# Plain chunks 9 to 7, pairs 19 to 20, weight sums from the second chunk on, and some early transfers moved

## The chip, the cores and the metric

The kernel runs on one core of one Trainium2 chip. Its time is the device time in microseconds (us) of one execution. Before the change it is 2727.89 us, the median of three runs (2726.22 to 2728.48). The core has five engines that run at the same time, each with its own queue of instructions in a fixed order: TensorE (PE, matmuls), VectorE (DVE), ScalarE (ACT), GpSimd (POOL) and SyncE (SP, which here only issues DMAs). POOL issues DMAs as well, from its own queue.

## What is computed

Eight sequences of 3008 tokens with 256 channels go through a Fourier transform along the sequence, a complex 256x256 mix with soft thresholding of the spectrum, the inverse transform, and a gated feed-forward network (256 to 1536 to 256) on all 24064 tokens.

```python
X = np.fft.rfft(x, axis=1)
Yr = Xr @ w_r - Xi @ w_i + b_r
Yi = Xr @ w_i + Xi @ w_r + b_i
Y = sign(Y) * maximum(abs(Y) - 0.01, 0)        # real and imaginary part apart
y = np.fft.irfft(Y, n=3008, axis=1).reshape(24064, 256)
gate = 1 / (1 + np.exp(-(y @ w_gate)))
out = (gate * (y @ w_val)) @ w_out
```

## The kernel before, in words

**FFT.** 3008 is 47 x 64, so the transform is two stages with a store to DRAM and a load between them. Stage one is `fwd_a` for one of eight row groups of a batch (a *first-stage unit*: load `xf`, matmuls, copy, store to `zd`; `store_a` issues the store as two DMAs of 192 KB). Stage two, mix and inverse stage one run in *steps* `(q, b)`: `fwd_b(q)`, `mix(q - 1)`, `inv_b(q - 2)`. A step loads `zf` and a table `mf_sb`, and an inverse table `mi_sb` (two buffers, `NME`). Inverse stage two is `inv_a(u)`, an *inverse unit*: it loads `vf` and gives 376 tokens. The batches go in groups of 1, 1, 2, 2, 2 (`GROUPS`).

**Feed-forward network, plain.** The first T0 = `NPL` x 512 tokens go in chunks of 512 (`CW`). A chunk has 12 *units* (`ffn1`, `ffn2`; f is a block of 128 of the 1536 hidden features). A unit is 12 matmuls of 512 columns for gate and value (each a three-term product of high and low halves) and 6 for the output of an earlier unit: 18. On VectorE it has two operations (L465, L474), on ScalarE two (L463, L473).

**Feed-forward network, in pairs.** The other tokens go two chunks at a time (`half`, `second`): the gate and value products are made as 2x2 block products with 7 in place of 8 multiplications. A pair has 12 halves of 7 x 3 matmuls and 12 x 12 for the output. This needs sums of weight blocks, which `make_t` makes on POOL: 12 passes, each with two buffers of the ring `big` (five buffers, shared with `xf` of the first stage) and a store to `td`.

**Order.** The first block (manual order) transforms batch 0, converts weights and starts batch 1. Chunk 0 runs in manual order beside the first stage of batches 2 and 3 (`halves`) and the rest of the weight conversion. From chunk 1 on, a list `side` holds the remaining FFT work (steps, first-stage and inverse units, with weights such as 3.6 for a full step and 1.0 for a first-stage or inverse unit). After every unit the pace `rates` is added to `acc`, and side work is taken from the list as long as `acc` covers its weight. All of `side` but the last sixteen inverse units is spread over the units from 12 up to `len(ffn) - LAST_GAP` (20). Outside the manual blocks a scheduler orders each engine's instructions. Matmul results go to a ring of six PSUM banks (`RING`). At the end of the last chunk the FFT's buffers are given up, and the pairs start.

A VectorE step is, by line: L287 and L290 (operand of the mix), L308, L312, L313 (sum after the mix), L296 (threshold, after ScalarE's L295) and L319 (low half, after ScalarE's L318).

Of the kernel before, what the change touches and what calls it, by code (L numbers as in the profile page):

```python
# [22 lines left out]
LAM = float(np.float32(0.01))  # L23
GROUPS = (1, 1, 2, 2, 2)
CW = 512
NPL = 9
HW = 512
RING, L2_BANKS = 6, 2

# [8 lines left out]
EARLY = 4  # L38
# [71 lines left out]
def tile_fft_mix_ffn(ctx: ExitStack, tc, x, w_r, w_i, b_r, b_i, w_one, w_out, mf, mi, mis, fa, fb, mf0, fa0, out):  # L110
    nc = tc.nc
# [819 lines left out]
    def load_halves(b, u):  # L931
        for c in range(2):
            load_half(b, 2 * u + c)
# [11 lines left out]
    with tc.manual_schedule():  # L945
        for h in range(na):
            load_a(0, h)
        load_a(1, 0)
        for h in range(na):
            fwd_a(0, h)  # L950
            store_a(0, h)
            if h in (1, 3, 4):
                load_a(1, {1: 1, 3: 2, 4: 3}[h])
            if h == 2:
                load_mix()
        mfs[0] = load_mf(0, mf0)
        for q in range(2):
            load_b(0, q)
        mfs[1] = load_mf(1, mf0)
        load_bias4()  # L960
        load_part()
        mfs[2] = load_mf(2, mf0)
        for h in range(EARLY):
            fwd_a(1, h)
            if h == 1:
                wi_sb = mix_weights()
        keep_warm(bank("warm"), zero[:, :P], zero, WARM_Z)
        for q in range(NP + 2):
            if q + 2 < NP:
                load_b(0, q + 2)  # L970
            if 0 <= q - 1 < NP:
                mis_[q - 1] = load_mi(q - 1, True)
            if q < 2:
                for h in range(q * EARLY // 2, (q + 1) * EARLY // 2):
                    store_a(1, h)
            if q == 3:
                nc.sync.dma_start(fb_sb, fb)
                load_bias()
            if q % 2 and q <= NP:
                load_part()  # L980
            if q % 2 == 0 and 4 <= q < 4 + 2 * (na - EARLY):
                load_a(1, EARLY + q // 2 - 2)
            if q < NP:
                fwd_b(0, q, mfs[q], True)
            if q + 3 < NP:
                mfs[q + 3] = load_mf(q + 3, mf0)

            if q < NP:
                convert(q)
            if q == 4:  # L990
                sub(bias_sb[:, 1], bias_sb[:, 1], bias_sb[:, 0])
            if 0 <= q - 1 < NP:
                mix4(0, q - 1)
            if q == NP + 1:
                for bu in beside[:NR2K // 2]:
                    load_halves(*bu)
            if 0 <= q - 2 < NP:
                inv_b(0, q - 2, mis_[q - 2], True)
        steps = [convert_a, convert_b, convert_c]
        for h in range(EARLY, na):  # L1000
            fwd_a(1, h)
            store_a(1, h, nc.gpsimd)
            if steps:
                steps.pop(0)()
        for bu in beside[:AT_FIRST]:
            halves_a(*waiting.pop(0))
        for t in ("hi lo", "power mant one", "sum word", "hi lo"):
            ops(t, 0)
    p0s.close()
    p3 = p3s.enter_context(tc.tile_pool(name="p3", bufs=2, side="right", reuse_waits="tile"))  # L1010
    with tc.manual_schedule():
        for u in own0:
            load_v(u)
        load_part()
        for bu in beside[NR2K // 2:NR2K // 2 + AT_FIRST]:
            load_halves(*bu)
        for f in range(NF):
            ffn[f]()
            if parts:
                load_part()  # L1020
            if f in (2, 3):
                tables[f - 2, 1] = load_mi(f - 2, False, later=True)
            if f in (5, 6):
                keep_mi(f - 5, tables[f - 5, 1])
            halves(AT_FIRST + (f + 1) * (len(beside) - AT_FIRST) // NF)
# [49 lines left out]
    for j in range(NF, len(ffn)):  # L1075
        c, f = divmod(j, NF)
        ffn[j]()
        acc += rates[j >= part]
        if ts and c >= 3 and f % 4 == 1:
            make_t(*ts.pop(0))  # L1080
        while side and (acc >= side[0][0] or j >= (part if len(side) > n_last else end) - 1):
            if len(side) == n_last and j < part:
                break
            acc -= side[0][0]
            side.pop(0)[1]()
            if len(side) == n_last:
                fft.close()
                p4 = ctx.enter_context(tc.tile_pool(name="p4", bufs=1, reuse_waits="tile"))
                th, tl = (p4.tile([P, NH, 2, 3, P], F32R, name=t) for t in ("th", "tl"))
                spare += [p4.tile([P, 2, HW], F32R, tag="xop", bufs=NCB, name="spare") for _ in range(BEHIND)]  # L1090
                prep = list(PREP)
                to_load = list(range(NH))
                acc = 0.0
        if p4 and to_load and j % 2:
            load_t(to_load.pop(0))
        if c == NPL - 1:
            if f == 0:
                load_y(0)
            if f % 2:
                load_t1(f // 2)  # L1100
            if prep and f > 2:
                operand(0, prep[0])
                split(0, prep.pop(0), sub)
# [74 lines left out]
```

## Time and profile before

| | before |
|---|---|
| median of 3 runs | 2727.89 us |
| profiled execution, its own time | 2728.32 us |
| its span, first to last instruction | 2726.2 us |
| mean granted clock of TensorE | 0.997 |
| DMA packets, data | 170552, 241.48 MB |
| HBM read, written | 134.19 MB, 104.33 MB |

The busy time of each engine in 40 slices of the span, in tenths (9 is 90% or more), shows the stages: up to slice 2 the start, up to slice 15 the plain chunks with the FFT beside them, then the pairs.

```profile
PE   8899999999999999999999999999999999999999
DVE  5777778677777448777777777777777877777776
ACT  4666565555555444444444444444444444444443
POOL 0231001216000003333333324333333333333321
DMA  9887645777555660000000000000000000000000
```

The 1.0 for a full TensorE clock and the DMA share are means over a window; a wait is the idle time of an engine just before an instruction, put down to what released it last.

### The profile page before, as it was taken

How to read it: one execution, taken by the hardware profiler on the slowest of the kernel's cores; microseconds unless marked ns; L12 is line 12 of the kernel's file. 1: busy time of each engine (PE TensorE's matmuls, PEld its weight loads, DVE VectorE, ACT ScalarE, POOL GpSimd, SP SyncE). 2: the span in 40 equal slices, each digit the busy share in tenths (PEclk: the TensorE clock that was granted, in tenths of full speed). 3: DMA queues.
4: the chain of work that ended last, by engine and by line, in shares of the span. 5: the costliest groups of instructions: out<-in, count | busy, mean ns of one | idle time of the engine just before them, and what ended most of it. 6: DMA issues, size and time to landing. Idle time of an engine off the chain costs nothing.

```text
span 2726.2 us, 45298 instructions
## 1 busy us (share of the span) xinstructions
PE 2702.6 (99%) x17371; PEld 2240.3 (82%) x17371; DVE 2041.4 (75%) x3013; ACT 1353.3 (50%) x2373; POOL 727.8 (27%) x673
## 2 busy tenths in 40 slices
PE   8899999999999999999999999999999999999999
PEld 6668888888899888888888888888888888888887
DVE  5777778677777448777777777777777877777776
ACT  4666565555555444444444444444444444444443
POOL 0231001216000003333333324333333333333321
PEclk9999999999999999999999999999999999999999
DMA  9887645777555660000000000000000000000000
GB/s 279 256 247 200 185 136 173 205 211 213 167 161 155 191 182 9 31 31 16 16 31 32 16 16 31 31 26 7 31 32 31 2 31 31 31 16 16 32 16 16
DMA packets 170552, 241.48 MB, mean 89 GB/s; under 512 B 17184, under 2 KB 127648, under 8 KB 170336
## 3 DMA queue, kind: packets, MB, share of 16 engines
q1 hardware_dynamic: 159664, 215.18, 26.3%
q0 software_dynamic: 10416, 23.34, 2.7%
q8 instruction: 137, 2.24, 0.4%
q14 instruction: 79, 0.65, 0.1%
q10 hardware_dynamic: 256, 0.07, 0.0%
HBM read 134.19 MB, written 104.33 MB: 87 GB/s over the span
## 4 chain that ended last, share of the span: by engine, by line
PE 95%; DMA 2%; DVE 2%; ACT 1%; issue 0%; SPq 0%; POOL 0%; ACTq 0%; DVEq 0%
PE pc L717 11%; PE pd L717 11%; PE pa L717 11%; PE po L693 8%; PE po L692 8%; PE po L694 8%; PE pm L306 6%; PE pb L717 6%; PE pb L272 3%; PE pia L393 2%; PE pg L457 2%; PE pg L458 2%; PE pg L459 2%; PE pv L457 2%; PE po L485 2%; PE pv L458 2%
## 5 line engine op out<-in xcount | busy, mean ns | idle before, releaser
L775 POOL TENSOR_TENSOR c<-c,c 128x512 f32<-128x512 f32 x114 | 147.3, 1292 | 779.2 <-DVE c L771 588.4
L692 PE MATMUL po<-hh,w 128*128 128x512 f32 x912 | 354.8, 389 | 0.0
L693 PE MATMUL po<-hh,w 128*128 128x512 f32 x912 | 354.8, 389 | 0.0
L694 PE MATMUL po<-hl,w 128*128 128x512 f32 x912 | 354.8, 389 | 0.0
L717 PE MATMUL pc<-s,w1h 128*128 128x512 f32 x912 | 280.9, 389 | 0.0
L717 PE MATMUL pa<-a,w1h 128*128 128x512 f32 x912 | 280.8, 389 | 0.0
L771 DVE TENSOR_TENSOR c<-u,pc 128x512 f32<-128x512 f32 x228 | 156.7, 687 | 91.1 <-PE pc L717 85.3
L746 DVE TENSOR_TENSOR u<-u,pb 128x512 f32<-128x512 f32 x228 | 155.4, 681 | 91.2 <-PE pb L717 61.2
L664 ACT CAST hh<-v 128x512 fp32r<-128x512 f32 x114 | 70.7, 620 | 305.7 <-DVE v L756 305.7
L668 POOL TENSOR_TENSOR hl<-c,hh 128x512 fp32r<-128x512 f32 x114 | 152.4, 1337 | 186.1 <-ACT hh L664 186.1
L717 PEld LDWEIGHTS pc<-s,w1h 128*128 128x128 f32 x912 | 171.1, 188 | 35.7 <-DVE v L748 0.2
L692 PEld LDWEIGHTS po<-hh,w 128*128 128x128 f32 x912 | 171.2, 188 | 35.6
L694 PEld LDWEIGHTS po<-hl,w 128*128 128x128 f32 x912 | 171.2, 188 | 35.6
L717 PEld LDWEIGHTS pa<-a,w1h 128*128 128x128 f32 x912 | 171.2, 188 | 35.6
L693 PEld LDWEIGHTS po<-hh,w 128*128 128x128 f32 x912 | 171.2, 188 | 35.4
L306 PE MATMUL pm<-w_sb,xsh 128*128 128x256 f32 x1008 | 187.2, 287 | 1.2 <-ACT xsh L289 0.8
L717 PE MATMUL pc<-s,w1l 128*128 128x512 f32 x456 | 177.4, 389 | 0.0
L717 PE MATMUL pa<-a,w1l 128*128 128x512 f32 x456 | 177.4, 389 | 0.0
L750 DVE TENSOR_TENSOR v<-v,pd 128x512 f32<-128x512 f32 x228 | 156.8, 688 | 24.4 <-DVE v L748 0.9
L777 DVE TENSOR_TENSOR u<-u,pd 128x512 f32<-128x512 f32 x228 | 156.8, 688 | 24.5 <-DVE c L771 0.9
L748 DVE TENSOR_TENSOR v<-u,pc 128x512 f32<-128x512 f32 x228 | 156.8, 688 | 24.1 <-PE pd L717 0.5
L742 ACT COPY u<-pa 128x512 f32<-128x512 f32 x228 | 133.9, 587 | 70.2 <-PE pa L717 70.0
(185 smaller groups left out, 6620.7 us busy)
## 6 DMA issues: line engine op xcount, KB each, us to landing
zf<-zd SPq DMA_DIRECT2D x96, 256.0 KB, 3.4
vf<-vd SPq DMA_DIRECT2D x128, 192.0 KB, 3.9
out_dram<-ot SPq DMA_DIRECT2D x93, 256.0 KB, 2.2
vd<-vz SPq DMA_DIRECT2D x85, 256.0 KB, 2.9
ypair<-yd SPq DMA_DIRECT2D x19, 1024.0 KB, 4.9
yd<-yf SPq DMA_DIRECT2D x103, 188.0 KB, 3.4
xf<-in_x_dram SPq DMA_DIRECT2D x80, 192.0 KB, 4.4
zd<-xf SPq DMA_DIRECT2D x72, 192.0 KB, 2.9
```

The lines of the kernel that those rows point to most:

```text
L306: nc.tensor.matmul(o, l, r, start=(i == 0), stop=(i == len(mms) - 1))
L668: sub_(hl, h, hh)
L692: nc.tensor.matmul(o, wh, hh, start=(f == 0), stop=False)
L693: nc.tensor.matmul(o, wl, hh, start=False, stop=False)
L694: nc.tensor.matmul(o, wh, hl, start=False, stop=(f == NF - 1))
L717: nc.tensor.matmul(o, l, r, start=not more and l is wh and r is xh, stop=l is wl, skip_group_check=more)
L746: add(u, u, b)
L748: add(v, u, c)
L750: add(v, v, d)
L771: add(c12, u, c)
L775: nc.gpsimd.tensor_mul(c12, g12, c12)
L777: add(u, u, d)
```

## The change

```diff
-NPL = 9
+NPL = 7
...
-            if 0 <= q - 1 < NP:
-                mis_[q - 1] = load_mi(q - 1, True)
+            for i in (0, 1) if q == 1 else (q - 1,) if 2 < q <= NP else ():
+                mis_[i] = load_mi(i, True)
...
         for h in range(EARLY, na):
             fwd_a(1, h)
-            store_a(1, h, nc.gpsimd)
+            if h == EARLY:
+                store_a(1, h, nc.gpsimd)
             if steps:
                 steps.pop(0)()
...
         for bu in beside[NR2K // 2:NR2K // 2 + AT_FIRST]:
             load_halves(*bu)
+        for h in range(EARLY + 1, na):
+            store_a(1, h)
         for f in range(NF):
             ffn[f]()
...
-        if ts and c >= 3 and f % 4 == 1:
+        if ts and c >= 1 and f % 4 == 1:
             make_t(*ts.pop(0))
```

There are 7 plain chunks (84 units) and 20 pairs, where there were 9 (108 units) and 19. The side work up to the last sixteen inverse units, with weights of 369.4 in sum (372.4 after: three inverse units move from the chunks' own list to it), is spread over 52 units, where it was 76: `rates` is 372.4 / 52 = 7.16 a unit, where it was 369.4 / 76 = 4.86. Passes of `make_t` follow units 13, 17, 21 and so on to 57, where they followed 37, 41 and so on to 81. In the first block the tables `mi_sb` of q = 0 and 1 are loaded together. The stores of three first-stage units of batch 1 (h = 5, 6, 7) move from POOL to SP, behind the first loads of chunk 0.

SyncE, at the start of chunk 0, in the change against before (`xfh` is the input of `halves`, `vf` that of an inverse unit, `raw` a piece of the weights to be converted, `zd_84` the first-stage result of batch 1):

```order
 L865 DMA raw<-in_w_out_dram 128x1024
 L168 DMA xfh<-in_x_dram 48x512 x4
+L168 DMA zd_84<-xf 48x1024 x6
 L168 DMA vf<-vd_91 48x1024 x2
 L865 DMA raw<-in_w_one_dram 128x1024
```

The six stores are new on SP here; on POOL, `zd_84<-xf` falls from eight to two.

VectorE in the FFT of batch 1, before: from one unit of the network (L465) to the next.

```order
L465 TENSOR_TENSOR sg<-sg,pv 128x512
L296 SCALAR_TENSOR_TENSOR yc<-ys,yc 128x512
L474 TENSOR_TENSOR hl<-sg,hh 128x512
L319 TENSOR_TENSOR yl<-yc,yh 128x512
L287 TENSOR_TENSOR xsf<-xsf 128x2x128
L308 TENSOR_TENSOR yt<-pm,bias_sb 128x512
L290 TENSOR_TENSOR xsl<-xsf,xsh 128x768
L312 TENSOR_TENSOR ys<-pm_2289,yt 64x256
```

The same place in the change; the rows begin inside the first of two steps.

```order
L287 TENSOR_TENSOR xsf<-xsf 128x2x128
L308 TENSOR_TENSOR yt<-pm,bias_sb 128x512
L296 SCALAR_TENSOR_TENSOR yc<-ys,yc 128x512
L290 TENSOR_TENSOR xsl<-xsf,xsh 128x768
L319 TENSOR_TENSOR yl<-yc,yh 128x512
L312 TENSOR_TENSOR ys<-pm_2448,yt 64x256
L313 TENSOR_TENSOR ys<-yt 64x256
L312 TENSOR_TENSOR ys<-pm_2448,yt 64x256
L313 TENSOR_TENSOR ys<-yt 64x256
L296 SCALAR_TENSOR_TENSOR yc<-ys,yc 128x512
L319 TENSOR_TENSOR yl<-yc,yh 128x512
L465 TENSOR_TENSOR sg<-sg,pv 128x512
```

Two steps now stand between two units, where one stood, and L313, L296 and L319 of the second step follow each other directly, with a ScalarE operation between each two of them.

GpSimd in the change, among the inverse tables of the second FFT (`mi_sb` loaded, then kept in `md`; `tb` and `tr` are the buffers of `make_t`):

```order
L253 DMA mi_sb<-in_mis_dram 128x2x256
L588 TENSOR_TENSOR tb<-w1h,w1l 128x256 x2
L590 TENSOR_TENSOR tb<-tb 128x128
L591 TENSOR_TENSOR tb<-tb 128x128
L592 TENSOR_TENSOR tb<-tb 128x128
L593 TENSOR_TENSOR tb<-tb 128x128
L259 DMA md<-mi_sb 128x2x256
L253 DMA mi_sb<-in_mis_dram 128x2x256
```

Before, all tables stand ahead of the first `tb`; now one pass lies between two of them, and the one of unit 13 lies among the stores of chunk 0.

## The prediction

> **What bounds the kernel now.** I read the page first (engine shares, chain), then TensorE's (PE's) own waits, then two windows: the stage in which FFT steps run between the plain units, and the stage of the pairs.
>
> ```profile
> span 2726.2 us, 45298 instructions
> PE 2702.6 (99%) x17371; PEld 2240.3 (82%) x17371; DVE 2041.4 (75%) x3013; ACT 1353.3 (50%) x2373; POOL 727.8 (27%) x673
> PE 95%; DMA 2%; DVE 2%; ACT 1%; issue 0%; SPq 0%; POOL 0%; ACTq 0%; DVEq 0%
> ...
> PE pia L393 <- issue: 3.2, 1, 3.2
> PE pia L393 <- DMA vf<-vd: 2.4, 3, 1.4
> PE pi L348 <- DMA mi_sb<-in_mi_dram: 1.8, 2, 1.6
> ...
> 640.00:670.00 30.00, 30.00 (x306) 25.15 (x299) 24.34 (x33) 16.19 (x30) 23.38 (x36) 1.00 0.68 209
> 670.00:700.00 30.00, 29.56 (x359) 24.61 (x358) 23.64 (x39) 17.74 (x34) 11.89 (x19) 1.00 0.80 227
> 700.00:730.00 30.00, 29.37 (x355) 25.86 (x354) 20.11 (x36) 17.11 (x30) 0.00 (x0) 1.00 0.59 165
> 190.00:905.00 715.00, 713.73 (x7083) 614.62 (x7083) 547.18 (x930) 422.57 (x734) 101.34 (x152) 1.00 0.62 178
> 1400.00:2000.00 600.00, 600.00 (x2649) 496.82 (x2648) 471.56 (x643) 271.43 (x473) 206.85 (x155) 1.00 0.06 22
> ```
>
> The window columns are PE, weight loads, VectorE (DVE), ScalarE (ACT), GpSimd (POOL), clock, DMA share, GB/s. PE is busy all the way and makes 95% of the chain, so a matmul less is time less, as long as nothing else becomes late. In the pairs 2649 matmuls take 600 us: **0.2265 us each**. The rows of waits (total, times, longest) are small, and those shown lie in the first 110 us: a table, an input of the first inverse units, and an unexplained `issue`. In the plain stage (190 to 905 us) PE is busy 713.73 of 715. VectorE comes second there, 547 us; it is the engine to watch when that stage is squeezed.
>
> **Two plain chunks become a pair.** A plain chunk issues 12 x 18 = 216 matmuls of 512 columns, two of them 432. A pair issues 12 halves x 7 products x 3 = 252 and 12 x 12 = 144 for the output, 396. So 36 fall away: 36 x 0.2265 = **-8.15 us**. The FFT, its inverse and the weight sums keep their number of instructions.
>
> **The two inverse tables.** PE waits for the second table after its operand is long ready:
>
> ```profile
> 49.73 0.45 PE L348 MATMUL pi<-yc,mi_sb 128*128 128x256 f32 x1 [1.58 <-DMA mi_sb<-in_mi_dram]
> ```
>
> It is issued behind four stores; moved ahead of them, some 5 us earlier, it lands before PE asks for it. These stores, one raw load and a table behind them go out later by one issue, some 0.5 us, and nobody waits for them there. Bounds 0 and -1.8 (both waits of that row's kind); I take **-1.6**.
>
> **The six stores (three units).** They leave POOL at 98 to 102 us, while the first inverse units wait for their input:
>
> ```profile
> 98.15 2.07 POOL L168 DMA_DIRECT2D zd<-xf  x4 [1.09 <-ACT xf L203]
> 101.45 1.02 POOL L168 DMA_DIRECT2D zd<-xf  x2 [1.24 <-ACT xf L203]
> ...
> zd<-xf SPq DMA_DIRECT2D x72, 192.0 KB, 2.9
> ...
> 100.00:110.00 10.00, 4.56 (x133) 3.61 (x132) 5.34 (x10) 5.14 (x10) 3.25 (x7) 0.70 0.98 325
> 110.00:120.00 10.00, 10.00 (x52) 6.32 (x52) 5.68 (x11) 6.79 (x12) 2.21 (x4) 0.79 0.43 123
> ...
> 102.60 1.15 PE L393 MATMUL pia<-fb_sb,vf 48*64 48x47 f32 x64 [1.44 <-DMA vf<-vd]
> 104.08 1.74 PE L393 MATMUL pia<-fb_sb,vf 48*64 48x47 f32 x54 [0.33 <-DMA vf<-vd]
> 109.03 0.46 PE L393 MATMUL pia<-fb_sb,vf 48*64 48x47 f32 x6 [3.22 <-issue]
> 109.96 0.80 PE L457 MATMUL pg<-yth,w1h 128*128 128x512 f32 x1 [0.46 <-ACT yth L381]
> 116.00 0.50 PE L457 MATMUL pg<-yth,w1h 128*128 128x512 f32 x1
> 120.09 0.50 PE L457 MATMUL pg<-yth,w1h 128*128 128x512 f32 x1
> ```
>
> Six transfers of 192 KB are 1.2 MB, 3.6 us at the 325 GB/s of that window. DMA is full (0.98) until 110 us and half empty (0.43) behind it; the stores now go out on SP at about 104 to 108 us, into that gap. Of the three PE waits here, 1.44 and 0.33 are for that input and 3.22 for nothing the profile shows (my reading: the next instructions, fetched through the same DMA). The first unit then takes 6.04 us (109.96 to 116.00), the second 4.09, at a clock of 0.79. Bounds: +3.7 if SP's next loads slip by as much as the stores take and PE waits for it, and -7 for all waits and the slow clock gone. I take the two input waits and a third of the 3.22: **-3.0**.
>
> The Trainium skill (TensorE: Matmul & The Clock Gate, "What's actually happening") says that the clock halves after one idle window of about 3.4 us; the 0.70 and 0.79 agree. By it the slow first unit, 2 us, would go too once the waits are short, and the sum would be 2 us lower; by the rows alone I leave it in.
>
> **The plain stage gets denser.** The 84 full FFT steps that lay between 76 units now lie between 52: the pace at which the kernel hands out side work rises from 4.86 to 7.16 of its weights a unit, so that a unit is followed by two steps where it was one. The stage loses 24 units, 24 x 4.08 = 98 us, of PE cover, and the side work keeps its size. PE's costs come from the starts of three units in a row: between the first two lie a unit, a step and a first-stage unit, between the last two a unit and a step. DVE's come from its groups in the window (busy and mean, then the idle time ahead and who ended it):
>
> ```profile
> 411.40 0.39 PE L457 MATMUL pg<-yth,w1h 128*128 128x512 f32 x1
> 420.45 0.40 PE L457 MATMUL pg<-yth,w1h 128*128 128x512 f32 x1
> 428.27 0.40 PE L457 MATMUL pg<-yth,w1h 128*128 128x512 f32 x1
> ...
> L290 DVE TENSOR_TENSOR xsl<-xsf,xsh 128x768 fp32r<-128x768 f32 x84 | 83.1, 989 | 8.7 <-ACT xsh L289 7.9
> L313 DVE TENSOR_TENSOR ys<-yt 64x256 f32<-64x256 f32 x168 | 77.1, 459 | 3.7
> L312 DVE TENSOR_TENSOR ys<-pm,yt 64x256 f32<-64x256 f32 x168 | 70.6, 420 | 7.8
> L296 DVE SCALAR_TENSOR_TENSOR yc<-ys,yc 128x512 f32<-128x512 f32 x84 | 59.7, 711 | 54.2 <-ACT yc L295 53.5
> L319 DVE TENSOR_TENSOR yl<-yc,yh 128x512 fp32r<-128x512 f32 x83 | 58.8, 708 | 26.9 <-ACT yh L318 26.4
> L308 DVE TENSOR_TENSOR yt<-pm,bias_sb 128x512 f32<-128x512 f32 x84 | 57.8, 688 | 10.1 <-PE pm L306 9.1
> L474 DVE TENSOR_TENSOR hl<-sg,hh 128x512 fp32r<-128x512 f32 x75 | 52.3, 698 | 20.9 <-ACT hh L473 20.1
> L465 DVE TENSOR_TENSOR sg<-sg,pv 128x512 f32<-128x512 f32 x75 | 51.6, 688 | 10.3 <-PE pv L459 4.3 <-ACT sg L463 3.8
> L287 DVE TENSOR_TENSOR xsf<-xsf 128x256 f32<-128x256 f32 x83 | 38.0, 457 | 24.0 <-ACT xsf L285 23.3
> ```
>
> On PE a unit is 18 x 0.2265 = 4.08 us, a step 7.82 - 4.08 = 3.74, a first-stage unit 9.05 - 7.82 = 1.23; an inverse unit I take as 1.1, from the row of 64 small matmuls at 102.60 (1.15). On DVE a step is the seven FFT groups, 445.1 / 84 = 5.30, a unit (L474, L465) 1.39; the groups add up to 563 with the small ones, the window has 547, so neighbours overlap by 3%: 5.15 and 1.35. Besides, DVE stands idle where it hands a tile to ACT and takes it straight back (L296, L319, L474): 102 us on the 133 places where the order leaves nothing between, 0.77 each. Before: 547 + 102 = 649 of 715, 91%. After, units 13 to 33 hold 36 steps, 18 first-stage and 9 inverse units and 44 such places: PE 85.7 + 134.6 + 22.1 + 9.9 = 252; DVE 185 + 28 + 4 + 34 = 251. Units 34 to 64 (48 steps, 14, 37, 67 places): PE 364, DVE 347. So for 250 us DVE has nothing to spare, and what hid it, PE's longer row of matmuls, is gone. PE is not stopped at once: its results lie in six PSUM banks, and an order with some slack in it takes up a short lead of one engine. But a lead that grows ends in PE waiting for a bank or for a split operand. The nearest place in the trace is 640 to 700 us, where GpSimd's sums slow DVE (24 of 30 busy): PE lost 0.44 and 0.63 us in 60 to 90. Over 252 us that is 3 to 4.5. Bounds 0 and +13 (rival 3); I take **+4.5**.
>
> **The weight sums** run from the second chunk on, five of twelve passes in units 13 to 33. What they cost DVE is in the means above. POOL also loads the second FFT's tables:
>
> ```profile
> 651.22 1.86 POOL L588 TENSOR_TENSOR tb<-w1h,w1l 128x256 f32<-128x256 f32 x2
> 659.51 1.44 POOL L588 TENSOR_TENSOR tb<-w1h,w1l 128x256 f32<-128x256 f32 x2
> ...
> 659.16 2.09 DVE L313 TENSOR_TENSOR ys<-yt 64x256 f32<-64x256 f32 x1
> ...
> POOL mi_sb L253 <- PE pi L353: 39.5, 10, 12.7
> ```
>
> One pass takes 8.3 us there (from one start to the next). In the order one lies between the tables of the second FFT, and one among the first chunk's stores. Behind it on POOL wait a table and its copy, and for the table PE's inverse product. POOL has 4 us in hand per table (39.5 over 10, waiting for a free buffer), and a table is asked for two steps, 7.5 us, after it could be issued; two passes could cost PE at most 2 x (8.3 - 4.0) = 8.6. DMA, busy 0.62 of 715 us, comes to 0.72 of 617 (715 - 98); at 0.80, in the row 670 to 700, PE lost 0.44. I take **+1.5** for both, near the lower end of 0 to +8.6, since the step ahead covers most of a pass.
>
> The Trainium skill (GPSIMD Engine Reference, "8. Key points") says that POOL shares its SBUF interfaces with DVE instructions of two SBUF inputs. The 2.09 us against a mean of 459 ns agrees that there is contention. What it would cost at its worst is rival 4; by the means of the groups it is inside the 5.15 and 1.35, and the sum stays as it is.
>
> **Sum.** -8.15 - 1.6 - 3.0 + 4.5 + 1.5 = -6.75. The profiled execution took 2728.32 us (2.1 around its span); 2728.32 - 6.75 = 2721.6. The median, 2727.89, lies 0.4 lower: **2721 us**.
>
> **Rivals.**
> 1. DVE keeps up and the start clears: -8.15 - 1.6 - 7 + 0 = 2711. For it: before, PE waited only some 3 us in 715. Against: no spare time in units 13 to 33.
> 2. The stores' move gains nothing (SP's loads slip, or the 3.22 stays): -8.15 - 1.6 + 0 + 6 = about 2724, no change to be told. That is the change not doing what it says. For it: the 3.22 has no named cause, and SP is a queue in order, whose next loads feed the first chunk.
> 3. Slower: DVE becomes the bound in units 13 to 33. If each place of direct return grows by 0.3 us, since ACT, at most 422.57 / 617 = 68% busy, is more often in the middle of another tile, 44 x 0.3 = 13 come on top: 2734. It decides (slower by more than 0.2%) from 12.2 / 44 = 0.28 us on. Against: the mean, 54.2 us over 67 places, is 0.81 with ACT at 59%.
> 4. Slower by more: GpSimd's sums stop DVE for as long as they run. Five passes of 8.3 us in the full units are 41 us: about 2762. Against: from 640 to 670 us POOL was busy 23.38 and DVE still 24.34 of 30.
>
> **How the numbers follow.** Forecast 0.40, of which 0.30 lies below 2722.4, the bound of 0.2% (5.5 us, about what a measurement of this kernel can tell from no change); rival 1 0.22; rival 2 0.23; rival 3 0.13, of which 0.02 within 0.2%; rival 4 0.02. Faster 0.30 + 0.22 = 0.52, same 0.10 + 0.23 + 0.02 = 0.35, slower 0.11 + 0.02 = 0.13. The range, 2711 to 2733, runs from rival 1 to just short of rival 3, and leaves out half of either end.
>
> **What would show it.** Right: no wait for the second table; less than 4 us of PE waits at 100 to 110 us; PE waits of 3 to 8 us in units 13 to 33, ended by DVE; 20 pairs at 89.7 us each. Wrong: PE waits there above 15 us or none; loads of tables waited for behind POOL's sums; new waits for loads in the first chunk.

## The result and the profile after

The changed kernel is slower: 2745.18 us, median of six runs (2743.36 to 2751.2), beside 2729.28 us for the kernel before on the same chip (six runs as well, the three shown ahead among them); ratio 1.0065, 95% interval 1.0054 to 1.0076. The profiled execution has a span of 2743.9 us, 17.7 us more than before.

The page of the changed kernel: span, busy time, two rows of the 40 slices, and the chain.

```profile
span 2743.9 us, 45406 instructions
PE 2708.0 (99%) x17335; PEld 2241.8 (82%) x17335; DVE 2072.8 (76%) x3052; ACT 1358.9 (50%) x2390; POOL 753.5 (27%) x690
...
DVE  5777777777883577778777777777777777787776
...
POOL 0242120221000133333333333333433333333321
...
PE 87%; DVE 7%; ACT 3%; DMA 2%; issue 1%; SPq 0%; POOL 0%; DVEq 0%; ACTq 0%
```

PE still looks 99% busy, but its share of the chain fell from 95% to 87%, and VectorE's (DVE's) rose from 2% to 7%: for some 5% more of the time than before, the end is set by DVE's work. GpSimd's (POOL's) peak of 6 tenths in slice 9 before (counted from 0) is now spread over slices 3 to 9.

PE's own waits in the same profile (total, times, longest):

```profile
PE pi L351 <- ACT yh L318: 6.6, 6, 2.8
...
PE pia L393 <- issue: 2.8, 2, 2.0
PE pb L272 <- DMA zf<-zd: 2.4, 2, 1.3
PE pm L306 <- DVE yt L308: 2.3, 1, 2.3
```

The same row in the plain stage of the kernel before (190 to 905 us):

```profile
PE pi L351 <- ACT yh L318: 0.3, 1, 0.3
```

The largest wait is new, 6.6 us in the whole run, 5.9 of them from 188 us on: the inverse product (L351) waits for the high half of the thresholded spectrum (L318), a link near the end of the chain of a step through DVE and ScalarE (ACT). These rows explain only part of the loss. The ends of matmuls are modelled, so a short gap between two of them is partly painted over, and after a longer one the clock is lower. I therefore measured each unit by its start: **time over the matmuls** is the time from a unit's first gate matmul to the next unit's, less the matmuls that the program puts between at their own durations (us each, fitted to units 14 to 85 before: network 0.2305, mix 0.1146, inverse product 0.1234, first FFT product 0.2396, first stage 0.288, an inverse unit 1.2).

| us over the matmuls | start of unit 13 | units 13 to 20 | 21 to 33 | 34 to 44 | 45 to 64 | later units | sum |
|---|---|---|---|---|---|---|---|
| before | 190.68 | 0.0 | 2.1 | 0.0 | 0.9 | 3.7 | 6.5 |
| changed | 188.35 | 16.5 | 8.8 | 1.0 | 8.9 | 0.8 | 35.9 |

From the last plain unit's start to the end of the span it is 1716.8 us before and 1806.9 after, so the pair that was added takes 90.2; the 24 plain units that went took 24 x 18 x 0.2305 = 99.6. Together: 90.2 - 99.6 = -9.4, the start -2.3, the FFT stage 35.9 - 6.5 = +29.4, in sum +17.7, which is the difference of the spans. The loss is all in units 13 to 64.

How such a loss arises, in the timeline of the changed kernel (start, duration, engine, operation, then the idle time before it and who ended it):

```profile
214.17 1.94 DVE L313 TENSOR_TENSOR ys<-yt 64x256 f32<-64x256 f32 x1
...
214.38 1.44 POOL L588 TENSOR_TENSOR tb<-w1h,w1l 128x256 f32<-128x256 f32 x2
...
216.12 0.43 DVE L312 TENSOR_TENSOR ys<-pm,yt 64x256 f32<-64x256 f32 x1
...
217.17 0.73 ACT L295 ACTIVATE yc<-ys,ebias 128x512 f32<-128x512 f32 x1 [2.29 <-DVE ys L313]
...
218.38 0.68 DVE L296 SCALAR_TENSOR_TENSOR yc<-ys,yc 128x512 f32<-128x512 f32 x1
...
219.09 0.62 ACT L318 CAST yh<-yc 128x512 fp32r<-128x512 f32 x1 [0.47 <-DVE yc L296]
...
219.76 0.39 PE L351 MATMUL pi<-yh,mi_sb 128*128 128x256 f32 x1 [1.77 <-ACT yh L318]
```

L313, 0.42 us elsewhere, takes 1.94 while POOL makes two of its sums. L312, which reads PSUM, keeps its 0.43. ACT then waits 2.29 us for L313, and PE 1.77 us for ACT. The windows of such places (PE, weight loads, DVE, ACT, POOL, clock, DMA share, GB/s):

```profile
206.60:225.30 18.70, 16.93 (x97) 12.19 (x94) 13.44 (x21) 8.69 (x15) 6.38 (x11) 0.86 0.66 195
...
611.40:627.30 15.90, 13.42 (x148) 12.06 (x148) 12.95 (x16) 6.57 (x13) 14.18 (x24) 1.00 0.77 238
```

DVE is not full in the first (13.44 of 18.70), and the clock falls to 0.86; in the second POOL works for 14.18 of 15.90 us, and 16 DVE operations take 12.95.

### The profile page after: what moved, and what is told of

It is laid out like the page before. It is cut to its first block, busy times and chain, and to the rows that moved or that the text cites. A ratio compares the mean times of both kernels' runs of the same rounds, so it can differ in the third digit from the quotient of the medians.

```text
span 2743.9 us, 45406 instructions
## 1 busy us (share of the span) xinstructions
PE 2708.0 (99%) x17335; PEld 2241.8 (82%) x17335; DVE 2072.8 (76%) x3052; ACT 1358.9 (50%) x2390; POOL 753.5 (27%) x690
## 3 DMA queue, kind: packets, MB, share of 16 engines
q1 hardware_dynamic: 161680, 218.46, 26.4%
q0 software_dynamic: 10032, 22.16, 2.5%
## 4 chain that ended last, share of the span: by engine, by line
PE 87%; DVE 7%; ACT 3%; DMA 2%; issue 1%; SPq 0%; POOL 0%; DVEq 0%; ACTq 0%
PE pa L717 12%; PE pc L717 12%; PE pd L717 12%; PE po L694 8%; PE po L693 8%; PE po L692 8%; PE pb L717 6%; PE pm L306 4%; PE pb L272 2%; PE pia L393 2%; PE pg L457 1%; PE pa L201 1%; PE pg L458 1%; PE pv L457 1%; PE pg L459 1%
## 5 line engine op out<-in xcount | busy, mean ns | idle before, releaser
L692 PE MATMUL po<-hh,w 128*128 128x512 f32 x960 | 373.5, 389 | 0.0
L693 PE MATMUL po<-hh,w 128*128 128x512 f32 x960 | 373.5, 389 | 0.0
L694 PE MATMUL po<-hl,w 128*128 128x512 f32 x960 | 373.4, 389 | 0.0
L717 PE MATMUL pa<-a,w1h 128*128 128x512 f32 x960 | 295.7, 389 | 0.0
L717 PE MATMUL pc<-s,w1h 128*128 128x512 f32 x960 | 295.6, 389 | 0.0
L717 PEld LDWEIGHTS pa<-a,w1h 128*128 128x128 f32 x960 | 180.1, 188 | 37.7 <-DVE sg L465 0.4
L717 PEld LDWEIGHTS pc<-s,w1h 128*128 128x128 f32 x960 | 180.1, 188 | 37.6 <-DVE v L748 0.2
L692 PEld LDWEIGHTS po<-hh,w 128*128 128x128 f32 x960 | 180.2, 188 | 37.4
L693 PEld LDWEIGHTS po<-hh,w 128*128 128x128 f32 x960 | 180.2, 188 | 37.4
L694 PEld LDWEIGHTS po<-hl,w 128*128 128x128 f32 x960 | 180.2, 188 | 37.4
L306 PE MATMUL pm<-w_sb,xsh 128*128 128x256 f32 x1008 | 187.3, 287 | 3.3 <-DVE yt L308 2.3
L717 PE MATMUL pa<-a,w1l 128*128 128x512 f32 x480 | 186.8, 389 | 0.0
L717 PE MATMUL pc<-s,w1l 128*128 128x512 f32 x480 | 186.8, 389 | 0.0
```

The costliest lines, as they stand in the source:

```text
L306: nc.tensor.matmul(o, l, r, start=(i == 0), stop=(i == len(mms) - 1))
L692: nc.tensor.matmul(o, wh, hh, start=(f == 0), stop=False)
L693: nc.tensor.matmul(o, wl, hh, start=False, stop=False)
L694: nc.tensor.matmul(o, wh, hl, start=False, stop=(f == NF - 1))
L717: nc.tensor.matmul(o, l, r, start=not more and l is wh and r is xh, stop=l is wl, skip_group_check=more)
```

## The experiments

Three theories stood against each other. A: the results of a step pass DVE and ACT for longer than a step takes on PE, and where two steps of one and the same batch stand between two units, PE comes too early. B: DVE is full. C: the arithmetic of the weight sums stops DVE. Line numbers of the later kernels are a few higher than those of the change (L307 for L306, L353 for L351). The table gives each run's time and its time over the matmuls, as above; the ratios with their intervals stand with the runs. Each row is one profile. The run with the start as before, whose plain stage is that of the change, has a sum of 32.0 us in place of 35.9, so some 4 us between two rows can be scatter.

| kernel | us, median | start of unit 13 | units 13 to 20 | 21 to 33 | 34 to 44 | 45 to 64 | later | sum |
|---|---|---|---|---|---|---|---|---|
| sums' arithmetic out (e2) | 2735.86 | 197.94 | 8.3 | 2.6 | -0.9 | 4.9 | 0.7 | 15.5 |
| the same, buffers kept (f2) | 2729.83 | 192.79 | 8.3 | 3.7 | -0.9 | 3.7 | 0.9 | 15.8 |
| slower pace for batch 1 (e3) | 2745.70 | 190.75 | 2.6 | 5.7 | 5.1 | 19.5 | 0.4 | 33.3 |
| both (g1) | 2733.28 | 187.15 | 0.0 | 2.8 | 1.0 | 17.8 | 0.3 | 22.0 |
| both, loads earlier (i1) | 2723.86 | 190.04 | 0.0 | 2.8 | 1.3 | 6.8 | 0.6 | 11.4 |
| sums late (f1) | 2738.92 | 188.47 | 8.3 | 2.6 | 2.6 | 14.2 | 0.8 | 28.4 |
| sums in chosen units (g2) | 2742.29 | 192.25 | 10.0 | 3.4 | 3.2 | 13.9 | 1.2 | 31.7 |
| side work over 58 units (f3) | 2756.82 | 187.79 | 9.3 | 1.1 | 5.7 | 0.7 | 31.3 | 48.1 |
| the same, sums later (f4) | 2757.74 | 191.52 | 4.9 | 0.8 | 3.8 | 3.6 | 30.2 | 43.2 |
| nine chunks, sums early (e1) | 2732.41 | 190.93 | 1.3 | 3.5 | 0.1 | 0.2 | 6.0 | 11.1 |
| nine, arithmetic out (g3) | 2726.76 | 193.41 | 0.0 | 2.1 | 0.0 | 0.2 | 3.2 | 5.4 |

**Nine chunks with the rest of the change.**

```diff
-NPL = 7
+NPL = 9
```

> The change with nine plain chunks in place of seven: the moved transfers at the start and the weight sums from the second chunk on stay, the denser plain stage goes. Theory A (the loss comes from two FFT steps of one and the same batch between two units: a step's results pass VectorE and ScalarE for longer than the 3.74 us of a step): the units 13 to 33 lose nothing, the start keeps its 2.3 us, 2726 to 2728 us. Theory B (VectorE is full, because the stage is shorter): the same. Theory C (the weight sums beside the second FFT slow VectorE and hold up its tables, at any density): 2735 to 2740 us.

2732.41 us, ratio 1.0015 (1.0006 to 1.0024). Theories A and B expected 2726 to 2728, C 2735 to 2740; it fell between. Without the denser stage the rest of the change still loses 4.8 us, less than C said.

**The arithmetic of the sums left out.** GpSimd stores `w1h` in their place.

```diff
-            g.tensor_add(b[:, k], w1h[:, f, i], w1l[:, f, i])
...
+        nc.gpsimd.dma_start(td[fp, i], w1h[:, f0:f0 + 2].bitcast(F32).rearrange("p f i t n -> p (f i t n)"))
```

> The change with the arithmetic of the weight sums left out (GpSimd only stores w1h in their place, so the pairs compute with wrong weights). Theory A: little of the loss goes, 2738 to 2744 us. Theory B: VectorE is freed of its slowed operations only, 2738 to 2744 us. Theory C: most of the loss goes, 2722 to 2730 us.

2735.86 us, ratio 1.0026 (1.0017 to 1.0035). Some 10 us of the loss went. In the units it is 20.4 of 35.9; the time shows less of it because the first chunk came out 9.6 us later in this kernel's profile (unit 13 at 197.94). With no arithmetic and no buffer to wait for, GpSimd issued all twelve stores of 512 KB by 182 us, before unit 13, and from 100 to 187 us DMA was 0.93 busy at 302 GB/s, where the change has 0.82 and 250; that is the likely reason, and the run with the buffers kept (below) does not have it. Theory C expected the place right and the total too low; what is left, 15.5, is not the sums.

**A slower pace for the FFT of batch 1 alone.** `phase1` is the first part of `side`, `w1` its weights.

```diff
+    slow = (w1 / N1, (rates[0] * (part - NF) - w1) / (part - NF - N1))
...
-        acc += rates[j >= part]
+        acc += rates[1] if j >= part else slow[j >= NF + N1]
```

> The change with another pace: the FFT of batch 1 alone is spread over ten units (about 4.8 a unit, as before the change), all later side work over the other 42 (about 7.7 a unit). Theory A: the waits of units 13 to 18 (15 us over the matmuls' own time) go, the later phases, with two batches in turn, lose 1 to 4 us more: 2729 to 2735 us. Theory B: the later units are fuller still, so what is won in the first ten is lost there: 2743 to 2750 us. Theory C: no great change, 2740 to 2746 us.

2745.7 us, ratio 1.0064 (1.0052 to 1.0077): no gain, as B said. But the units say more: 13 to 20 fell from 16.5 to 2.6, as A said, and 10.6 us came in one single unit, 50.

**The start as before.**

```diff
-            for i in (0, 1) if q == 1 else (q - 1,) if 2 < q <= NP else ():
-                mis_[i] = load_mi(i, True)
+            if 0 <= q - 1 < NP:
+                mis_[q - 1] = load_mi(q - 1, True)
...
-            if h == EARLY:
-                store_a(1, h, nc.gpsimd)
+            store_a(1, h, nc.gpsimd)
...
-        for h in range(EARLY + 1, na):
-            store_a(1, h)
```

> The change with the start as before (six stores on GpSimd, tables one by one). The unit 13 started 2.3 us earlier in the change, so all theories of the plain stage expect 2.3 us more, 2746 to 2749 us. If the start's edits shift later work as well (stores of batch 1 behind SyncE's loads, so that its FFT starts with its input late), 2735 to 2742 us.

2745.44 us, ratio 1.0063 (1.0049 to 1.0077), against 1.0065 (1.0054 to 1.0076) with the start changed: between the two expectations, and no difference that can be told. The two intervals leave room for some 5 us, so this run alone does not exclude the 2.3. The starts of unit 13 say more. It starts at 189.78 us here and at 190.68 in the kernel before. Of the eighteen kernels with the new start, seventeen have it from 187.15 to 193.41, median 190.4; the other, at 197.94, is the one whose stores all went out before. The 2.3 us in the profile of the change are inside this scatter, and a gain of 4.6, as foretold, would show in the median.

**The sums late; the sums' buffers kept.** The first moves the twelve passes to units 37, 39 to 59; the second leaves their arithmetic out but keeps both buffers and the store, so that the loads of the first stage wait for them as before.

```diff
-        if ts and c >= 1 and f % 4 == 1:
+        if ts and c >= 3 and f % 2 == 1:
```

> The change with the twelve weight sums after units 37, 39 to 59 in place of 13, 17 to 57: out of the second FFT with its tables on GpSimd and out of the FFT of batch 1 alone, at the same density of FFT steps, twice as thick. Theory C1 (a pass slows VectorE's operations on two SBUF inputs, and in a full unit PE pays some 1.7 us for each pass, wherever it lies): 2741 to 2747 us. Theory C2 (the passes cost only where they lie in units 13 to 33: behind tables of the second FFT, or in the chain of a lone batch): units 13 to 33 lose 7 us in place of 25, 2726 to 2734 us. Theory B (VectorE full by the density alone): 2743 to 2748 us.

```diff
-            g.tensor_add(b[:, k], w1h[:, f, i], w1l[:, f, i])
...
+        nc.gpsimd.memset(w[:, 0, :1], 0.0)
...
+        nc.gpsimd.dma_start(r.bitcast(F32), w1h[:, f0:f0 + 2].bitcast(F32).rearrange("p f i t n -> p (f i t n)"))
```

> The change with the arithmetic of the weight sums left out, but their two buffers and their store kept (a DMA fills the buffer with w1h, so the pairs compute with wrong weights). Theory C (GpSimd's arithmetic slows VectorE): units 13 to 64 lose 10 to 15 us over the matmuls' own time in place of 35, 2722 to 2729 us. Theory D (the sums hold buffers for which SyncE's loads of the first stage wait, and all loads behind them): 2740 to 2746 us, as the change.

Late sums: 2738.92 us, ratio 1.004 (1.0027 to 1.0053), between C1 and C2. Units 13 to 33 lose 10.9 as without sums, units 34 to 64 lose 16.8 where they lose 2.8 without: the cost went along with the passes. Buffers kept: 2729.83 us, ratio 1.0001 (0.9991 to 1.001); the units agree with the run without buffers to 0.3 us in the sum. So theory D, loads held up by the buffers, falls: the arithmetic is the price, 35.9 - 15.8 = **20.1 us**. VectorE's groups show it, from 188 to 836 us (units 13 to 63 of the change), in the changed kernel and then in the run with the buffers kept (busy, mean ns, idle before):

```profile
L290 DVE TENSOR_TENSOR xsl<-xsf,xsh 128x768 fp32r<-128x768 f32 x84 | 84.1, 1001 | 5.5 <-ACT xsh L289 4.7
L313 DVE TENSOR_TENSOR ys<-yt 64x256 f32<-64x256 f32 x168 | 77.8, 463 | 3.8
L312 DVE TENSOR_TENSOR ys<-pm,yt 64x256 f32<-64x256 f32 x168 | 70.6, 420 | 7.3 <-PE pv L459 0.5 <-DVE yt L308 0.5
L296 DVE SCALAR_TENSOR_TENSOR yc<-ys,yc 128x512 f32<-128x512 f32 x84 | 58.3, 694 | 44.3 <-ACT yc L295 43.4
...
L319 DVE TENSOR_TENSOR yl<-yc,yh 128x512 fp32r<-128x512 f32 x83 | 57.6, 694 | 25.6 <-ACT yh L318 25.0
L287 DVE TENSOR_TENSOR xsf<-xsf 128x256 f32<-128x256 f32 x83 | 38.3, 462 | 21.2 <-ACT xsf L285 20.5
L474 DVE TENSOR_TENSOR hl<-sg,hh 128x512 fp32r<-128x512 f32 x51 | 37.9, 743 | 18.3 <-ACT hh L473 18.0
L465 DVE TENSOR_TENSOR sg<-sg,pv 128x512 f32<-128x512 f32 x51 | 35.1, 688 | 8.5 <-PE pv L459 4.7 <-ACT sg L463 2.6
```

```profile
L290 DVE TENSOR_TENSOR xsl<-xsf,xsh 128x768 fp32r<-128x768 f32 x84 | 80.0, 953 | 5.5 <-ACT xsh L289 4.7
L313 DVE TENSOR_TENSOR ys<-yt 64x256 f32<-64x256 f32 x168 | 70.7, 421 | 3.8
L312 DVE TENSOR_TENSOR ys<-pm,yt 64x256 f32<-64x256 f32 x168 | 70.6, 420 | 6.6
L296 DVE SCALAR_TENSOR_TENSOR yc<-ys,yc 128x512 f32<-128x512 f32 x84 | 58.0, 690 | 43.1 <-ACT yc L295 42.2
...
L319 DVE TENSOR_TENSOR yl<-yc,yh 128x512 fp32r<-128x512 f32 x84 | 57.8, 688 | 25.6 <-ACT yh L318 24.1 <-PE pb L272 0.8
L465 DVE TENSOR_TENSOR sg<-sg,pv 128x512 f32<-128x512 f32 x55 | 37.9, 688 | 22.4 <-PE pv L459 17.9 <-ACT sg L463 3.3
L474 DVE TENSOR_TENSOR hl<-sg,hh 128x512 fp32r<-128x512 f32 x54 | 37.3, 691 | 20.4 <-ACT hh L473 20.1
L287 DVE TENSOR_TENSOR xsf<-xsf 128x256 f32<-128x256 f32 x84 | 35.5, 422 | 21.2 <-ACT xsf L285 20.5
```

Four groups with two SBUF inputs are clearly shorter without the sums (L313 by 42 ns, L290 by 48, L474 by 52, L287 by 40); the two others (L296, L319) differ by 4 and 6 ns. Those that read PSUM are the same to 1 ns (L312, L465). The means hide single long ones: of the 168 runs of L313 in the change 18 take over 0.1 us longer than the median of 0.42, the longest 1.94; without the arithmetic the longest is 0.43. 168 x 0.042 + 84 x 0.048 + 51 x 0.052 + 83 x 0.040 = 17 us of DVE time. In the kernel before, L313 and L290 were stretched as much (459 and 989 ns), and PE hardly felt it: its units lose 6.5 us, and 5.4 in the nine chunks without arithmetic.

**Side work over 58 units in place of 52**, then the same with the sums at units 25 to 69.

```diff
-LAST_GAP, SIDE_GAP = 20, 3
+LAST_GAP, SIDE_GAP = 14, 3
```

> The change with the side work up to the last sixteen inverse units spread over 58 units in place of 52 (6.42 a unit in place of 7.16), those sixteen over 11 units. Theory B (density): the loss of 30 us in units 13 to 64 falls by a third or more, 2732 to 2738 us. Theory C alone (the passes at any density above that of before): 2742 to 2745 us. If the last inverse units and the loads of the pairs' weights get too tight: up to 2748 us.

```diff
-        if ts and c >= 1 and f % 4 == 1:
+        if ts and c >= 2 and f % 4 == 1:
```

> As the run before, with the passes of the weight sums after units 25, 29 to 69 (from the third chunk on), so that none lies in the FFT of batch 1 alone. Theories B and C2 together: 2726 to 2732 us. Theory C1: 2734 to 2740 us.

2756.82 us, ratio 1.0106 (1.0089 to 1.0123), and 2757.74 us, ratio 1.0102 (1.0087 to 1.0117): both misses on the whole. Up to unit 64 density did what B said, 16.8 in place of 35.2 us and 13.1 with the sums later. But the sixteen inverse units, now on 11 units in place of 17, lost 30 us, with PE waiting for their input, up to 2.7 us at a time in the first run and 2.9 in the second. The last stage had no room to give.

**Slower pace without arithmetic; sums in chosen units; nine chunks without arithmetic.** The first joins two edits shown above, the third as well.

> The slower pace for the FFT of batch 1 alone (ten units, then 7.7 a unit) together with the sums' arithmetic left out (buffers and stores kept, so the pairs compute with wrong weights). Without the arithmetic the units 13 to 20 lost 8.3 of some 16 us, the same in two runs. Theory A (steps of a lone batch follow each other too closely): these 8.3 us go and the later units do not lose what they won: 2718 to 2724 us. Theory B (a full VectorE at 7 weights a unit): units 21 to 64 lose more than before by as much, 2727 to 2733 us.

```diff
-        if ts and c >= 1 and f % 4 == 1:
+        if ts and j in (21, 25, 35, 37, 39, 41, 43, 53, 55, 57, 59, 61):
```

> The change with the twelve weight sums only after units 21, 25, 35 to 43 and 53 to 61, where the profiles of the change and of the run with late sums lost least by them. Theory C1 (a pass costs the same wherever it lies in the full stage, 1.2 to 1.7 us): 2740 to 2746 us. Theory C3 (a pass costs only where FFT steps have no slack: the FFT of batch 1 alone, and the ends of the later FFTs): 2728 to 2734 us.

> Nine plain chunks, the start as in the change, the sums from the second chunk on, but without their arithmetic (buffers and stores kept, so the pairs compute with wrong weights). Beside the nine chunks with the arithmetic (2732.4 us): if the arithmetic alone slows the FFT at the old density too, 2726 to 2728 us; if what those lost is due to the stores and buffers coming earlier, 2731 to 2733 us.

The pace takes units 13 to 20 from 8.3 to 0.0 us, and units 13 to 33 from 12.0 to 2.8. PE's queue of weight loads shows these gaps better than the matmuls do; first the run with buffers kept, then the one with the slower pace, each from unit 13 to 290 us:

```profile
PEld pi L352 <- DVE yl L319: 3.4, 5, 0.8
PEld pi L351 <- ACT yh L318: 3.1, 6, 1.0
```

```profile
PEld pi L353 <- DVE yl L320: 1.2, 3, 0.8
...
PEld pi L352 <- ACT yh L319: 0.3, 1, 0.3
```

6.5 us of waits for the two halves of the spectrum became 1.5. So theory A holds for these 8.3 us. In the median, 2733.28 us, ratio 1.0015 (1.0005 to 1.0024), the pace did not pay, since unit 50 lost its 10.6 us again. The sums in chosen units: 2742.29 us, ratio 1.0045 (1.003 to 1.006), as C1 had it. But GpSimd does not run them where the text has them; it starts as soon as its buffers come free. The last five passes, placed after units 53 to 61, ran at 589 to 640 us, in units 44 to 48, so the run does not test C3 for them. Nine chunks without arithmetic: 2726.76 us, ratio 0.9992 (0.9982 to 1.0001); the units lose 5.7 us less than with it (5.4 and 11.1): the early sums cost at the old density too, a quarter of what they cost at the new one.

**The sums behind the FFT**, in buffers of the pairs' operands, every second pass on VectorE: seven chunks, nine, and seven with the slower pace for batch 1 over ten and over eight units.

```diff
-        g = nc.gpsimd
-        w = big("tb").rearrange("p (a b) n -> p a b n", a=2)
+        g = nc.vector if i else nc.gpsimd
+        w = p4.tile([P, 2, HW], F32R, tag="xop", bufs=NCB, name="tb").bitcast(F32)
...
-        if ts and c >= 1 and f % 4 == 1:
+        if ts and p4:
             make_t(*ts.pop(0))
```

> The change with the weight sums moved out of the FFT: after units 64 to 75, where only inverse units lie beside the network, every second one on VectorE, in buffers of the pairs' operands; all results right. Theory C (the arithmetic costs only where FFT steps leave VectorE no slack): the 20 us that the sums cost go, and 15.8 us over the matmuls' own time stay in the FFT: 2723 to 2728 us. If the sums now hold up the last units or the pairs' first weights: up to 2740 us.

> Nine plain chunks, the start as in the change, the sums in the same place near the end of the plain chunks (units 88 to 99). At the old density the arithmetic cost 5.7 us from the second chunk on and about 1 us from the fourth chunk on: 2724 to 2728 us; if the new place itself costs, as much more here as in the run before.

> As the first of these, with the FFT of batch 1 alone spread over ten units. In the run with this pace and without arithmetic the 8.3 us of units 13 to 20 went, but a wait of 10.6 us came at unit 50 (a load of zf that comes late at the change from one FFT to the next). Same place, same wait: 2729 to 2734 us. If that wait hung on what GpSimd did there (the stores of the sums share the DMA queues): 2718 to 2723 us.

> As the run before, with eight units for the FFT of batch 1 alone (6.0 a unit, then 7.4). Theory A: a step apart is enough for most of the 8.3 us, and the order at unit 50 is that of the change again: 2717 to 2723 us, faster than the kernel before. Theory B (any pace loses the same somewhere): 2725 to 2732 us.

2743.1 (ratio 1.0057, 1.004 to 1.0074), 2742.53 (1.0055, 1.004 to 1.007), 2747.37 (1.0068, 1.0053 to 1.0083) and 2745.68 us (1.0065, 1.005 to 1.008). All lose in the new place: units 65 to 82 lose 14.2 to 15.3 us with seven chunks, and with nine units 89 to 106 lose 18.3, where the same nine chunks without arithmetic lose 1.6. A window of the nine chunks shows what stands against PE there:

```profile
930.00:940.00 10.00, 6.41 (x138) 4.86 (x137) 9.90 (x17) 1.86 (x4) 9.19 (x15) 0.83 0.87 267
```

With half of the passes on DVE, DVE is full there (9.90 of 10.00) and POOL too (9.19); PE falls to 6.41 and the clock to 0.83. In the FFT all went as expected: 8.3 us in units 13 to 20 with the even pace, 0.0 with ten units, 5.6 with eight. Unit 50 lost 10.4 us again with ten units, so it does not hang on what GpSimd did there. The page gives GpSimd's DMAs a queue of their own, too: q0, 22.16 MB in this run and in the change, 28.45 with the twelve copies of the run with the buffers kept, while q1 stays at 218.46.

**The first loads of an FFT earlier.** What stands at unit 50 is the change from one FFT to the next. Its first loads stand on SyncE behind loads and stores of inverse units. In the run with the slower pace and no arithmetic, SyncE and then PE:

```profile
642.46 1.03 SPq L240 DMA_DIRECT2D mf_sb<-in_mf_dram  x2
...
644.59 0.50 SPq L265 DMA_DIRECT2D zf<-zd  x1
```

```profile
650.43 2.04 PE L273 MATMUL pb<-mf_sb,zf 128*128 128x128 f32 x8 [6.15 <-DMA zf<-zd]
```

PE waits 6.15 us and then runs its eight matmuls in 2.04 us in place of 1.05: the granted clock is 0.50 from 650.5 to 658 us. With a second wait of 0.93 us for `zf`, the unit loses 10.6.

```diff
+    for t, g in zip(phases, groups[2:]):
+        t.insert(len(t) - 5, (0.0, begins[g[0]]))
```

`begins` issues the first `mf_sb` and `zf` loads of a group, `phases` are the four parts of `side`. The first run has this with the slower pace and without arithmetic; the second has the sums in full, six passes after units 51 to 61 and six after 64 to 74, on GpSimd alone.

> The run with the slower pace for batch 1 and without the sums' arithmetic (wrong weights in the pairs), and in addition the first zf and mf_sb loads of each later FFT issued some five entries of the list of side work earlier. If the 10.6 us at unit 50 are this one order of loads (the new FFT's first loads stand on SyncE behind vf loads and yd stores, and PE comes to them at once): they go, units 13 to 64 lose some 11 us, 2719 to 2725 us. Theory B (density loses them somewhere): 2729 to 2734 us.

> The same pace and loads with all results right: six passes of the sums after units 51 to 61, six on GpSimd alone after units 64 to 74, in buffers of the pairs' operands. With both passes at 51 to 61 and those behind 64 free: as the run before, 2719 to 2725 us, faster than the kernel before. If a pass costs its 1.2 us here too: 2734 to 2740 us.

```profile
636.38 0.46 SPq L240 DMA_DIRECT2D mf_sb<-in_mf_dram  x1
636.89 1.11 SPq L265 DMA_DIRECT2D zf<-zd  x2
```

The loads go out 6 to 8 us earlier, and unit 50 loses nothing: 2723.86 us, ratio 0.9981 (0.9972 to 0.999), faster than the kernel before by 5.6 us, but without the sums' arithmetic. Against the even pace (buffers kept), units 13 to 33 win 9.2 us and units 34 to 64, now denser, lose 5.3 more (8.1 in place of 2.8): the denser stage costs there, whether by DVE's load or by the chain is not shown. With the sums in full 2730.14 us, ratio 1.0004 (0.9995 to 1.0014), no difference from before: units 45 to 64 lose 13.7 us in place of 6.8. GpSimd took the first six passes and the beginning of a seventh up at 581 to 650 us, in units 46 to 50 and so before their place in the text; the others, at 826 to 858 us, cost nothing (0.3 us in units 65 to 82).

**All twelve passes behind the FFT**, on GpSimd alone. The loads of the finished sums (`load_t`) move with them, from units 65, 67, 69, 71, 75, 79 to 68, 71, 73, 76, 78, 81.

```diff
-SUMS_AT = (51, 53, 55, 57, 59, 61, 64, 66, 68, 70, 72, 74)
+SUMS_AT = tuple(range(64, 76))
...
-                operand(0, prep[0])
+                operand(0, prep[0], nc.vector)
```

> The slower pace for batch 1, the earlier first loads, and now all twelve passes of the sums behind the FFT (units 64 to 75), on GpSimd alone; the operands of the first pair that GpSimd made there go to VectorE. All results right. In the run before, the six passes behind unit 64 cost nothing and the six others, which GpSimd took up at units 46 to 50 already, 6.3 us. Theory C (a pass costs only where FFT steps leave VectorE no slack): 2720 to 2727 us, faster than the kernel before. If twelve passes in a row hold up the pairs' first weights or operands: 2728 to 2740 us.

2740.57 us, ratio 1.0035 (1.0021 to 1.0049): a miss. The FFT lost as little as in the run without sums (10.8 us up to unit 64), but units 65 to 82 lost 19.5. VectorE was mostly idle there (4.28 of 20 us busy in the window below), so it is not the old cause. SyncE's waits and PE's, from 815 to 940 us, and a window:

```profile
SPq L617 <- DMA td<-tr: 11.3, 3, 6.6
```

```profile
PE pia L395 <- DMA vf<-vd: 4.9, 2, 4.2
PE pg L459 <- ACT yf L407: 3.6, 1, 3.6
```

```profile
840.00:860.00 20.00, 15.06 (x199) 11.83 (x201) 4.28 (x5) 4.85 (x9) 19.23 (x35) 0.83 0.82 272
```

SyncE stood up to 6.6 us at the load of a sum that GpSimd had not stored yet, and the inputs of the inverse units (`vf`) and their stores (`yd`) stood behind it; PE then waited 4.2 us for `vf`. I had put the loads too early. With later loads it may work; that wasn't tried.

## Why the prediction was wrong

| term | predicted, us | shown, us | by |
|---|---|---|---|
| two plain chunks to a pair | -8.15 | -9.4 | starts of the units, both profiles |
| tables and stores at the start | -4.6 | about 0 | the run with the start as before, starts of unit 13 |
| denser plain stage | +4.5 | +9.3 | arithmetic left out: 15.8 - 6.5 |
| weight sums | +1.5 | +20.1 | with and without arithmetic: 35.9 - 15.8 |

The shown terms add up to +20.0, where the profiles differ by 17.7 and the medians by 15.9; the first of these has the 2.3 us of the start's scatter in it. The old place of the sums cost up to 1.1 us too (6.5 - 5.4), so that much of the last row belongs to density.

The step that failed is the one on **the weight sums**: "What they cost DVE is in the means above." The means were right, 459 ns for L313 before and 463 after, and the DVE time is nearly the same. The error was to spend it as a mean. A pass does not make every operation 10% longer, it holds up single ones, by up to 1.5 us for L313 in the change, in the middle of the chain from mix to inverse product. Where a unit's matmuls stood between two steps, PE had work for that time; where two steps stand together, it has none. By the nine chunks without and with arithmetic the early sums cost 5.7 us, 0.5 a pass on average; at the new density 20.1, 1.7 a pass. The place that I took as the nearest, 640 to 700 us before, had this cover still, and so its 0.44 and 0.63 us could not be scaled by length. The upper bound, 8.6, counted only tables that wait behind sums on POOL; no wait for such a table showed. Rival 4 had the mechanism, but as five passes that stop DVE for 41 us; at 1.7 us, a pass of 8.3 us costs a fifth of its length. The price is far from even. Units 14 and 15 of the change (206.6 to 241.3 us) lose 8.6 us, and 2.9 with the buffers kept; one pass was begun there, the one at 214.38, so it cost 5.7 us, two thirds of what rival 4 asked of a pass. In the run with the old start the same two units lose 5.5, so there it cost 2.6. Of the twelve passes of the change the first ran before unit 13, two in units 13 to 20 cost 8.2 us, and the nine others 11.9, 1.3 each. I had given rival 4 a chance of 0.02, because DVE's busy time beside POOL's looked unharmed: an operation that is held up counts as busy.

The Trainium skill (SBUF — State Buffer, "SBUF: two separate sides") says that an operation of GpSimd and one of DVE with two SBUF inputs take the pair of ports that they share one after the other, for a whole instruction, and do not share it. The rows agree that an operation is stopped and not slowed: L313 took 1.94 us beside two sums of 1.44 us together, which leaves 0.50, and L312, which reads PSUM, its usual 0.43. They differ in the length: L313 was held for two instructions in a row, though its record starts 0.21 us ahead of the first. It is a rule against this change that the prediction should have weighed by its longest single stop, not by the sum of stops.

**The denser stage**: the size was off by 4.8 us, inside the bounds, and the reason was another one. Its comparison of DVE's load with PE's (251 to 252 us) did not decide: without arithmetic, at the same density, units 21 to 44 lose 2.8 us in sum. 8.3 of the 9.3 us lay in the FFT of batch 1 alone, where steps that follow each other are of the same batch, and a unit less between them brings the wait. The order shown ahead of the prediction had just these rows. A slower pace there took the 8.3 us away, and brought a late load at unit 50, which earlier loads took away; 5.3 us came back in the denser units behind.

**The start**: the second table is not waited for any more, as foretold. But PE's waits for `zf` in the first block rose from 0.5 to 2.4 us and one for a later table came, 0.7 us, so that nothing is won there. The waits for `vf` and `issue` are these:

```profile
101.07 1.43 PE L393 MATMUL pia<-fb_sb,vf 48*64 48x47 f32 x64 [0.78 <-DMA vf<-vd]
103.48 1.35 PE L393 MATMUL pia<-fb_sb,vf 48*64 48x47 f32 x54 [0.98 <-DMA vf<-vd]
106.80 0.46 PE L393 MATMUL pia<-fb_sb,vf 48*64 48x47 f32 x6 [1.96 <-issue]
107.72 0.80 PE L457 MATMUL pg<-yth,w1h 128*128 128x512 f32 x1 [0.46 <-ACT yth L381]
...
114.94 0.50 PE L457 MATMUL pg<-yth,w1h 128*128 128x512 f32 x1
```

They add up to 3.7 us, as the prediction's mark of less than 4 had it, but the first unit takes 7.2 us in place of 6.0, and over all runs the start brings nothing that can be told: rival 2 was right in this. DMA is 0.91 busy up to 110 us, and what is won in one wait is lost in the next. One profile cannot tell 2 us there. (The prediction's own terms, 1.44, 0.33 and a third of 3.22, make 2.84 and not 3.0.)

**The pair**: the mechanism and nearly the size were right. A plain unit's matmul takes 0.2305 us from start to start, not the 0.2265 of the pairs. No load or table was newly waited for in the first chunk, as foretold; PE's waits in units 13 to 33, ended by DVE and ACT, were of the kind foretold, but 25.3 us by the starts in place of 3 to 8.

What stays open: what a pass costs at a given place, since it was 1.05 us with late sums (28.4 - 15.8 over twelve), 1.3 in the change behind unit 20 and 4.1 in units 13 to 20; why L296 and L319 were hardly held up; and why unit 13 started late, at 192.8 and 193.4 us, in two more of the runs without the arithmetic. No version with the sums in full was faster than the kernel before; the nearest was level with it.

## What to carry to other kernels

A stall is priced by what covers it at its place, not by a mean. Before work is packed denser, look for the chain that goes through other engines and back, and compare its length with the work that is left between its two ends. An engine's busy time hides stops, since a stopped operation counts as busy; compare the same operation with and without the suspected neighbour. And measure a change part by part: here 9.4 us won, 9.3 lost by density and 20.1 by the sums lay in one number.

## What the runs showed of the hardware

VectorE operations with two SBUF inputs were held up by GpSimd's arithmetic, one for the length of two of its instructions in a row (L313, 0.42 to 1.94 us, beside 1.44), not only of one. Those that read PSUM kept their time (L312 420 ns, L465 688 ns, with the sums and without). In seventeen kernels with the same start, one profile each, unit 13 began between 187.15 and 193.41 us: with DMA at 0.86 in the first 190 us of the change, this start scatters by more than the 4.6 us that the edits to it were to bring. And two waits for loads, 6.15 and 0.93 us, cost 10.6 us, since the granted clock was 0.50 from 650.5 to 658 us behind the first: eight matmuls took 2.04 us in place of 1.05.
